# q and k read once in natural order, scores on four 64x64 tiles of TensorE, pooled scores on row tiles

## The chip, the cores and the metric

The kernel is one program on one core of a Trainium2 chip. A core has five engines that run lists of their own and meet through semaphores: TensorE (PE in the rows, with its weight loads as PEld), VectorE (DVE), ScalarE (ACT), GpSimd (POOL) and SyncE (SP), which issues every DMA here, one queue in order. Matmuls write PSUM, of which the kernel uses eight banks of 128 partitions by 512 fp32 columns. The metric is device time of one execution in microseconds, the median of several runs; lower is better.

## The reference

Attention of 8 batches, 8 heads, 576 positions, 64 dims, in two branches whose sum goes through a gated network. One branch averages q, k and v over groups of four positions and attends fully (144 x 144 scores); the other looks at a band of 7 keys around each query.

```python
q_d = q.reshape(B, H, Sd, 4, D).mean(axis=3)      # k_d, v_d alike; Sd = 144
out_up = np.repeat(sm_attn(q_d, k_d, v_d), 4, axis=2)
mask = np.abs(pos[:, None] - pos[None, :]) < 4
scores = np.where(mask, scale * np.matmul(q, k.transpose(0, 1, 3, 2)), -1e9)
out_local = np.matmul(softmax(scores), v)
x = (out_up + out_local) as (B * S, H * D)         # 4608 x 512
return (sigmoid(x @ w_gate) * (x @ w_val)) @ w_out # 512 -> 1536 -> 512
```

## The kernel before

A **unit** is one batch and two heads (32 units, four to a batch, numbered u = 0 to 31). A unit's attention is a chain of steps, each a small function in `unit_steps`:

- `prep2`: GpSimd sums groups of four columns of q and k (pooled q and k; k goes into a block tile `kdblk`, one half of partitions to a head, the rest zero).
- `s0`, `s1`: band scores. The 576 positions are cut into 10 blocks of 58 queries, each with 64 keys around it, and each block of each head is one 64x64x64 product in fp32, 20 to a unit, into two PSUM banks (tiles `s`). The host has laid q and k out twice: `qk`, in which the two partition halves hold even and odd blocks, cut and padded (a product of the lower half stands on rows and columns 0 to 63 of the array, one of the upper half on 64 to 127), and `qkd`, plain, with the two heads in the two partition halves, for pooling.
- `sm`, `a0`, `a1`, `v`, `x`: softmax, transposes and the product with v (tiles `x`). For the first six units (fp32, `plain`) v is copied by ScalarE into a block tile with zeros, and one 128x128x58 product serves a block of both heads. Later units use fp16 pairs and three passes.
- `d0`, `d1`, `dn`, `at`, `vd`, `od`: the pooled branch. `d0` and `d1` are one product each of pooled q (72 columns of it as weights, all 128 partitions) with `kdblk` (288 columns: both heads beside each other), tiles `sd`; after each, DVE takes row maxima and ScalarE two exponentials.

From a unit's output comes x. Batches 0 and 1 multiply it with w_gate and w_val as they are (`pg`, `pv`), while the weights are still being read, joined and split into fp16 pairs (`wload`, `wjoin`, `wsplit`); from batch 2 on seven products in place of eight are made from sums of weights (`pair`). `po` is the output product. All large products are fp16 in three passes of 288 columns.

**The order.** Every step has a place on one line, a number in the table `T` (`p0s0`, `m3d1` and so on); the steps are recorded in the order of their numbers, and a scheduler that knows the tiles then sets each engine's list. PSUM is two pools: five banks `mm` (products of the network, and everything of units 0 to 3) and three banks `att` (scores, pooled scores and transposes of later units). In units from 8 on the 20 band products are kept together; earlier they stand in groups of 12 and 8. While nothing else is to be done early, `awake` fills PE with idle products. Loads go through `load`, which keeps them in order on SP: for the first four units `qk`, mask, `qkd`, `vd` (pooled v), all four v, and so on by unit; `qk` has two buffers, `qkd` one (units 0 to 3 borrow room elsewhere).

Of the kernel before, what the change touches and what calls it, by code (L numbers as in the profile page):

```python
# [9 lines left out]
F16 = mybir.dt.float16  # L10
# [9 lines left out]
P = 128  # L20
# [5 lines left out]
R = 58  # L26
# [5 lines left out]
QR = 80  # L32
# [15 lines left out]
NSWAP = 8  # L48
NKD = 2
# [17 lines left out]
def attention_moe(ctx, tc, qk, qkd, v, vd, wg, wv, wo, mask, out):  # L67
# [53 lines left out]
    assert NRING * NBLOCK * KB + 4 * HN <= (NPC + 1) * WPC and 2 * XQ + 8 * HN <= (NPC + 1) * WPC and 3 * S + 8 * HN <= NST * 2 * WPC  # L121
# [18 lines left out]
    def borrowed(eng, i, n):  # L140
        t = borrow(i, n * P)
        eng.memset(t, 0.0)
        return t.rearrange("p (a b) -> p a b", a=n)

    vplain = [borrowed(nc.vector, 1, NBLK), borrowed(nc.gpsimd, 1, NBLK)]
    vdblk = [zeroed(nc.gpsimd, [P, NKC, P], F32, f"vdblk{i}") for i in range(2)]
    kdblk = [zeroed(nc.vector, [P, 2, SD], F32, f"kdblk{i}") for i in range(NKD)]
    adw = zeroed(nc.gpsimd, [QR, 2 * NKC * 2 * WIN], F32, "ad")
    ad = adw[:QM].rearrange("p (q c h k) -> p q c h k", q=2, c=NKC, h=2)
    ad16 = adw.bitcast(F16).rearrange("p (e q c h k) -> p e q c h k", e=2, q=2, c=NKC, h=2)  # L150
    vblk = cp.tile([P, 2, NBLK, P], F16, tag="vblk", name="vblk")
    vd16 = [t.rearrange("p c d -> p (c d)").bitcast(F16).rearrange("p (e c d) -> p e c d", e=2, c=NKC) for t in vdblk]
    flat = {id(vblk): vblk.rearrange("p t b c -> p (t b c)").bitcast(F32), id(adw): adw, **{id(t): t.rearrange("p c d -> p (c d)") for t in vdblk}}

    ones = cp.tile([P, 1], F32, tag="ones", name="ones")
    nc.vector.memset(ones, 1.0)
# [30 lines left out]
    def inv_scaled(dst, src, c):  # L187
        nc.vector.reciprocal(dst, src)
        nc.vector.tensor_scalar(out=dst, in0=dst, scalar1=c, scalar2=None, op0=ALU.mult)

    def absmax(dst, src):
        nc.vector.tensor_reduce(dst, src, axis=AX.X, op=ALU.max, apply_absolute_value=True)  # L192

    def split(hi, lo, src, sc):

        nc.scalar.activation(hi, src, AF.Copy, scale=sc)  # L196
        return nc.vector.scalar_tensor_tensor(out=lo, in0=src, scalar=sc, in1=hi, op0=ALU.mult, op1=ALU.subtract)  # L197


    mark = {}  # L200
# [157 lines left out]
    qkraw, qkdraw, vdraw = {}, {}, {}  # L358

    def load_qk(u):  # L360
        if 2 <= u < NPAIR:
            qkraw[u] = borrow(1, 2 * NJ * (R + WIN))
        else:
            qkraw[u] = raw.tile([P, 2 * NJ * (R + WIN)], F32, tag="qk", name=f"qk{u}", bufs=2)
        load(qkraw[u], qk[u])

    def load_qkd(u):
        if 1 <= u < NPAIR:
            qkdraw[u] = borrow(0, 2 * S)
# [15 lines left out]
    def first_loads():  # L385
        n = 0
        for u in range(NPAIR):
            load_qk(u)
            if u == 0:
                load(mk, mask)  # L390
# [773 lines left out]
```

## Time and profile before

| | us |
|---|---|
| median of 3 runs | 1016.58 (1010.73 to 1024.09) |
| profiled execution, its own time | 1018.99 |
| its span, first to last instruction | 1017.2 |
| first network product on PE | 63.4 |
| first product of batch 2's network | 340.5 |
| start of the last batch's network | 916.5 |

Before the first network product the attention of batch 0 and the first weights are prepared. From there to 150.4 us the network of batch 0 runs while the weights of the rest arrive; from 340.5 to 916.5 us five batches follow each other at about 115 us each; the last batch has no attention beside it.

### The profile page before, as it was taken

The page shows a single profiled execution, that of the slowest core. Times are in us where ns is not written, and L with a number is a line of the kernel's source. Part 1 is how long each engine was busy: PE and PEld are TensorE (multiplying, and loading weights), DVE is VectorE, ACT ScalarE, POOL GpSimd, SP SyncE. Part 2 cuts the span into 40 slices and gives each one's busy share as a digit, 9 for nine tenths or more (in the row PEclk, how much of TensorE's full clock was granted, in tenths as well). Part 3 has the DMA queues.
Part 4 walks back from the last instruction along what each step waited for, and adds up shares of the span by engine and source line. Part 5 has one row for each costly group of instructions (what it writes and reads, how often), then busy time and mean ns, then how long its engine had stood idle before and what let it go on. Part 6 is the DMA issues. An engine that isn't in the chain of part 4 may idle for free.

```text
span 1017.2 us, 23779 instructions
## 1 busy us (share of the span) xinstructions
PE 993.7 (98%) x9467; PEld 794.5 (78%) x9467; DVE 759.8 (75%) x1487; ACT 592.1 (58%) x1627; POOL 257.5 (25%) x309
## 2 busy tenths in 40 slices
PE   8999999999989999999999999999999999999998
PEld 6786677878778778878887777878778778887776
DVE  5968998576875899858895788857896588736850
ACT  5958778366763787535862676536863477322310
POOL 6400146523534322221402312221402311110000
PEclk9989999999999999999999999999999999999999
DMA  9548964333536557554855458555756455414501
GB/s 356 184 146 268 331 213 141 129 91 132 178 113 207 184 195 232 160 177 149 271 174 184 137 194 233 156 160 173 257 152 198 141 189 167 147 52 152 178 9 46
DMA packets 84735, 176.88 MB, mean 174 GB/s; under 512 B 44048, under 2 KB 50320, under 8 KB 84624
## 3 DMA queue, kind: packets, MB, share of 16 engines
q1 hardware_dynamic: 84624, 175.37, 52.7%
q8 instruction: 74, 1.21, 0.5%
q14 instruction: 37, 0.30, 0.1%
HBM read 147.03 MB, written 20.45 MB: 165 GB/s over the span
## 4 chain that ended last, share of the span: by engine, by line
PE 67%; DMA 12%; DVE 7%; ACT 5%; POOL 5%; issue 2%; SPq 1%; POOLq 0%; ACTq 0%; DVEq 0%
PE po L439 23%; PE pv L439 17%; PE pg L439 17%; DMA qkd<-in_qkd_dram 3%; PE s L502 3%; DMA v<-in_v_dram 2%; PE x L439 2%; PE sd L439 2%; POOL arena L840 2%; DMA wd<-arena 2%; PE od L439 1%; DMA arena<-in_wo_dram 1%; DMA at<-hl 1%; DMA arena<-in_wv_dram 1%; DVE arena L849 1%
## 5 line engine op out<-in xcount | busy, mean ns | idle before, releaser
L439 PEld LDWEIGHTS <-arena 128*128 128x128 f16 x4176 | 405.7, 98 | 118.2 <-ACT arena L196 4.4
L439 PE MATMUL po<-gq,wo 128*128 128x288 f16 x2304 | 290.5, 286 | 3.2 <-DVE gq L197 1.4
L439 PE MATMUL pg<-arena 128*128 128x288 f16 x2088 | 277.7, 288 | 5.9 <-ACT arena L196 3.5
L439 PE MATMUL pv<-arena 128*128 128x288 f16 x2088 | 274.3, 286 | 0.1
L439 PEld LDWEIGHTS <-wo 128*128 128x128 f16 x2304 | 223.8, 98 | 62.0 <-issue 3.0
L893 DVE TENSOR_TENSOR arena<-pv,arena 128x288 f32<-128x288 f32 x252 | 106.7, 451 | 27.0 <-PE pv L439 20.0
L537 ACT ACTIVATE t<-t,mx 128x64 f32<-128x64 f32 x300 | 75.4, 334 | 37.0 <-DVE mx L533 36.9
L419 POOL TENSOR_TENSOR qkd<-qkd 128x576 f32<-128x576 f32 x29 | 38.3, 1320 | 207.8 <-DMA qkd<-in_qkd_dram 207.8
L893 DVE TENSOR_TENSOR arena<-pg,arena 128x288 f32<-128x288 f32 x180 | 76.0, 449 | 10.7 <-PE pg L439 8.0
L196 ACT ACTIVATE vblk<-v,svb 64x640 f16<-64x640 f32 x52 | 42.9, 824 | 52.6 <-PE x L439 47.7
L554 ACT ACTIVATE t<-t,sm 128x64 f32<-128x64 f32 x250 | 62.3, 336 | 4.4 <-DVE sm L551 3.7
L813 ACT ACTIVATE arena<-po,osc 128x288 f32<-128x288 f32 x32 | 15.3, 496 | 71.7 <-PE po L439 71.7
L197 DVE SCALAR_TENSOR_TENSOR vblk<-v,svb,vblk 64x640 f16<-64x640 f32 x52 | 53.8, 1034 | 3.3 <-ACT vblk L196 2.2
L811 DVE TENSOR_SCALAR arena<-po,osc 128x288 f32<-128x288 f32 x32 | 16.3, 512 | 51.2 <-PE po L439 51.1
L714 POOL TENSOR_TENSOR arena<-arena 128x288 f32<-128x288 f32 x12 | 9.6, 796 | 171.3 <-DVE arena L689 171.3
L589 ACT ACTIVATE e<-sd,mxd 72x144 f32<-72x144 f32 x128 | 47.0, 370 | 6.1 <-POOL ad L614 5.0
L439 PE MATMUL sd<-kdblk,qks 128*72 128x288 f32 x128 | 42.7, 415 | 4.1 <-POOL kdblk L421 2.1
L502 PEld LDWEIGHTS s<-qk 64*64 64x64 f32 x1200 | 38.2, 135 | 8.2 <-issue 5.1
L502 PE MATMUL s<-qk 64*64 64x64 f32 x1200 | 43.4, 221 | 1.2 <-ACT e L589 0.9
L421 POOL TENSOR_TENSOR qks<-qkd 128x144 f32<-128x144 f32 x29 | 15.2, 525 | 113.3 <-PE sd L439 112.9
L521 DVE SCALAR_TENSOR_TENSOR t<-s,mk 128x256 f32<-128x256 f32 (+1 forms) x64 | 30.3, 484 | 14.9 <-PE s L502 14.8
L192 DVE TENSOR_REDUCE vm<-v 128x1 f32<-128x640 f32 x32 | 25.9, 812 | 19.7 <-DMA v<-in_v_dram 19.6
(147 smaller groups left out, 1400.5 us busy)
## 6 DMA issues: line engine op xcount, KB each, us to landing
arena<-wd SPq DMA_DIRECT2D x72, 896.0 KB, 4.6
qk<-in_qk_dram SPq DMA_DIRECT2D x30, 610.0 KB, 5.2
qkd<-in_qkd_dram SPq DMA_DIRECT2D x29, 576.0 KB, 5.5
vd<-in_vd_dram SPq DMA_DIRECT2D x29, 384.0 KB, 4.7
v<-in_v_dram SPq DMA_DIRECT2D x32, 320.0 KB, 4.9
arena<-in_wg_dram SPq DMA_DIRECT2D x12, 512.0 KB, 4.9
arena<-in_wv_dram SPq DMA_DIRECT2D x12, 512.0 KB, 4.6
arena<-in_wo_dram SPq DMA_DIRECT2D x12, 512.0 KB, 5.5
```

The lines of the kernel that those rows point to most:

```text
L192: nc.vector.tensor_reduce(dst, src, axis=AX.X, op=ALU.max, apply_absolute_value=True)
L196: nc.scalar.activation(hi, src, AF.Copy, scale=sc)
L197: return nc.vector.scalar_tensor_tensor(out=lo, in0=src, scalar=sc, in1=hi, op0=ALU.mult, op1=ALU.subtract)
L419: nc.gpsimd.tensor_tensor(out=x[:, :, 0:2], in0=x[:, :, 0:2], in1=x[:, :, 2:4], op=ALU.add)
L439: nc.tensor.matmul(o, w[a], x[c], start=first and i == 0, stop=last and i == len(pairs) - 1)
L502: return nc.tensor.matmul(o, qkraw[u][ps, g * R : g * R + WIN], kw[ps, g], start=True, stop=True)
L521: nc.vector.scalar_tensor_tensor(out=s["t"][:, j0:j1, :], in0=s["s", j0][:, : n * 2 * WIN].rearrange("p (a b) -> p a b", a=n), scalar=-QKS ...
L537: nc.scalar.activation(t[:, g], t[:, g], AF.Exp, bias=mx[:, g : g + 1], scale=-1.0, **(dict(accum_out=s["sm"][:, g : g + 1]) if fl("acs", ...
L554: nc.scalar.activation(t[:, g], t[:, g], AF.Copy, scale=sm[:, g : g + 1])
L589: nc.scalar.activation(s["e"][:, qb, h, :], pt[:QM, h * SD : (h + 1) * SD], AF.Exp, bias=mx[:, h : h + 1], scale=QKSCALE / 16, accum_out=s ...
L840: whole = nc.gpsimd.tensor_tensor(out=x.rearrange("p (f c) -> p f c", f=2), in0=home[k][:, 2 * p : 2 * p + 2, 0], in1=home[k][:, 2 * p : 2 ...
L893: eng.tensor_tensor(out=dst_, in0=x, in1=y, op=ALU.add)
```

## The change

**Loads.** `qk` is no longer read. `qkd` is loaded once a unit into a buffer with 13 columns of zero padding behind q and behind k, and serves pooling and band scores. Three such buffers go round. The order of the first loads is now a list of numbers in `T`: q of unit 0, mask, pooled v of unit 0, q of unit 1, two weights, and so on, with v last.

**Band scores.** Partition half is now the head, and the block's parity decides the output half, so the 20 products of a unit stand on all four 64x64 tiles of the array: rows by head, columns by parity. Each head has its own bank. They are kept together in all units.

**Pooled scores.** `kdblk` is gone. Pooled q and k stay side by side, and each head is a product of its own on 64 rows (72 columns of weights, 144 columns moving), two of each head, four to a unit, issued together in `d0` into two banks; the maxima and exponentials of head 0 are `d0`, those of head 1 `d1`.

**Pooling.** Two GpSimd instructions in place of four.

**Values.** In units 0 to 5 v is used as it is loaded: 20 products of 64x64 by 58 columns in place of 10 of 128x128, and no copies by ScalarE. The block tile for later units is zeroed once at the start instead of twice later.

**Places.** Most numbers of `T` differ. In the early units some work is on other engines: units 1 and 3 subtract their maxima on GpSimd and take one exponential (10 before), unit 0 does the reverse, and unit 0's division of the pooled branch goes from ScalarE to GpSimd.

```diff
     def load_qk(u):
-        if 2 <= u < NPAIR:
-            qkraw[u] = borrow(1, 2 * NJ * (R + WIN))
...
+        if NQK <= u < NPAIR:
+            qkraw[u] = padded(borrow(1, QKW))
         else:
-            qkdraw[u] = raw.tile([P, 2 * S], F32, tag="qkd", name=f"qkd{u}", bufs=1)
-        load(qkdraw[u], qkd[u])
+            qkraw[u] = qkbuf[u % NQK if u < NPAIR else (u - NPAIR) % NQK]
+        own(qkraw[u], u)
+        load(qkraw[u].rearrange("p (a c) -> p a c", a=2)[:, :, :S], qkd[u].rearrange("p (a c) -> p a c", a=2))
...
         def prep2():
-            sum4([(ALL, s["qd"], slice(0, SD))] + [(ps, s["kd"][ps, h], slice(SD, 2 * SD)) for h, ps in enumerate(HALVES)], x, fl("pr", u))
...
+            nc.gpsimd.tensor_tensor(out=y, in0=x[:, :, :, 0:2], in1=x[:, :, :, 2:4], op=ALU.add)
+            nc.gpsimd.tensor_tensor(out=s["qks"].rearrange("p (a g) -> p a g", a=2), in0=y[:, :, :, 0], in1=y[:, :, :, 1], op=ALU.add)
...
+        def s_four():
+            mine(qkraw[u], u)
+            for h in range(2):
+                s["s", h] = bank(f"s_{u}_{h}")
...
+            def one(h, hs, g, ps):
+                o = s["s", h][ps, g // 2 * WIN : (g // 2 + 1) * WIN]
+                a = g * R
+                return nc.tensor.matmul(o, qkraw[u][hs, a : a + WIN], qkraw[u][hs, QW + a : QW + a + WIN], start=True, stop=True).ins
...
+            run = [lambda x=(h, hs, 2 * j + par, ps): one(*x) for j in range(NJ) for h, hs in enumerate(HALVES) for par, ps in enumerate(HALVES)]
+            joined(run[2:] + run[:2])
...
+        def sd_products():
+            for h in range(2):
+                s["sd", h] = bank(f"sd_{u}_{h}")
+            return [lambda qb=qb, h=h, hs=hs: nc.tensor.matmul(
+                s["sd", h][:QM, qb * SD : (qb + 1) * SD], s["qks"][hs, qb * QM : (qb + 1) * QM], s["qks"][hs, SD:], start=True, stop=True).ins
+                for qb in range(2) for h, hs in ((1, HALVES[1]), (0, HALVES[0]))]
...
+            if plain:
+                for i0, i1 in CUT:
+                    o(i0, ALL)
+                joined([lambda i=i, ps=ps: nc.tensor.matmul(o(i, ps), vraw[u][ps, i], s["at"][0][ps, i, :R], start=True, stop=True).ins
+                        for i in [8, 9] + list(range(8)) for ps in HALVES])
```

PE, the band scores of unit 12 before (`po_1_2_0` is an output product of batch 1; a row with x8 is eight such products):

```order
L439 MATMUL po_1_2_0_4354<-gq_111,wo16_110 128x288
L439 MATMUL od_11_4323<-adt16_11_4320,vdblk1_121 128x144 x3
L502 MATMUL s_12_3_4330<-qk12_4150 64x64 x8
L502 MATMUL s_12_0_4329<-qk12_4150 64x64 x12
L439 LDWEIGHTS wo16_110
```

and the same place now:

```order
L424 MATMUL od_11_4326<-adt16_11_4324,vdblk1_119 128x144 x3
L460 MATMUL s_12_1_4333<-qk2_142 64x64 x2
L460 MATMUL s_12_0_4332<-qk2_142 64x64 x2
L460 MATMUL s_12_1_4333<-qk2_142 64x64 x2
L460 MATMUL s_12_0_4332<-qk2_142 64x64 x2
```

The number behind `s_12_` is now the head; head 1 and head 0 take turns, two products each (even and odd block). So it is in units 0, 4, 8 to 14, 16 to 18 and so on; in ten units (1, 2, 3, 5, 6, 7, 15, 19, 23, 27) ten products of head 1 stand ahead of ten of head 0.

PE, the pooled scores of units 14 and 15 now, with the band scores of unit 15 between them (before, `sd_14_0` and `sd_14_1` were one product each, 24 weight loads and products apart):

```order
L474 MATMUL sd_14_1_5194<-qks_14_5047 72x144
L474 MATMUL sd_14_0_5193<-qks_14_5047 72x144
L474 MATMUL sd_14_1_5194<-qks_14_5047 72x144
L474 MATMUL sd_14_0_5193<-qks_14_5047 72x144
...
L460 MATMUL s_15_1_5415<-qk2_142 64x64 x10
L460 MATMUL s_15_0_5414<-qk2_142 64x64 x10
...
L474 MATMUL sd_15_1_5516<-qks_15_5330 72x144 x2
...
L474 MATMUL sd_15_0_5515<-qks_15_5330 72x144 x2
```

In units 10, 15, 19, 23 and 27 the two heads' pooled products stand apart like those of unit 15, with three or six products of the network between them; in units 2, 3, 4 and 6 two of head 1 stand directly ahead of two of head 0; in the others they alternate.

## Rows read from the trace of the kernel before

**Rows 1.** Windows: stretch, its length, busy us by engine, clock, DMA share, GB/s.

```profile
0.00:63.40 63.40, 58.52 (x543) 48.00 (x544) 48.51 (x109) 45.90 (x138) 27.18 (x43) 0.92 0.64 238
63.40:150.40 87.00, 82.82 (x681) 62.37 (x680) 76.01 (x167) 66.87 (x160) 13.50 (x15) 0.96 0.77 263
150.40:340.50 190.10, 182.70 (x1807) 146.14 (x1806) 137.81 (x267) 117.37 (x338) 85.17 (x81) 1.00 0.43 138
340.50:916.50 576.00, 572.47 (x5650) 460.63 (x5649) 444.30 (x845) 341.12 (x964) 131.67 (x170) 1.00 0.56 179
916.50:1017.20 100.70, 97.16 (x794) 77.38 (x791) 53.17 (x101) 20.83 (x28) 0.00 (x0) 1.00 0.28 97
```

**Rows 2.** Waits of PE: us in total, times, longest.

```profile
PE sd L439 <- POOL kdblk L421: 2.1, 1, 2.1
PE sd L439 <- POOL qks L421: 1.3, 2, 0.7
```

**Rows 3.** Timeline of PE in batch 3: start, busy us, group.

```profile
480.65 0.65 PE L439 MATMUL sd<-kdblk,qks 128*72 128x288 f32 x2
481.13 0.90 PE L439 MATMUL pv<-arena 128*128 128x288 f16 x6
...
491.39 1.38 PE L502 MATMUL s<-qk 64*64 64x64 f32 x40
492.71 2.38 PE L439 MATMUL pv<-arena 128*128 128x288 f16 x18
...
496.39 0.90 PE L439 MATMUL od<-adt,vdblk 128*128 128x144 f32 x6
497.13 0.65 PE L439 MATMUL sd<-kdblk,qks 128*72 128x288 f32 x2
```

**Rows 4.** Timeline of PE, the first 12 band products of unit 0.

```profile
6.32 0.91 PE L502 MATMUL s<-qk 64*64 64x64 f32 x24
7.17 0.39 PE L88 MATMUL awake<-idle 128*128 128x256 bf16 x2
```

**Rows 5.** Windows of L502 alone: stretch, length, PE, PEld; (x) counts those in flight.

```profile
491.39:491.41 0.02, 0.01 (x2) 0.02 (x2) 1.00 0.85 358
...
491.49:491.51 0.02, 0.02 (x4) 0.02 (x5) 1.00 3.40 1434
491.51:491.55 0.04, 0.04 (x4) 0.04 (x6) 1.00 1.27 538
491.55:491.57 0.02, 0.02 (x6) 0.02 (x6) 1.00 1.70 717
491.57:491.61 0.04, 0.04 (x6) 0.04 (x6) 1.00 0.85 358
```

**Rows 6.** Timeline of PE, the value products of unit 4.

```profile
150.54 1.45 PE L439 MATMUL x<-at,vblk 128*128 128x58 f32 x12
151.82 0.27 PE L167 MATMUL mxt<-ident,m1o 128*1 128x128 f32 x1
...
152.31 1.04 PE L439 MATMUL x<-at,vblk 128*128 128x58 f32 x8
153.29 0.38 PE L172 MATMUL mxt<-mxg,ones 1*128 1x1 f32 x2
```

**Rows 7.** Timeline of the front: the first units' pooled chain.

```profile
7.90 1.15 POOL L419 TENSOR_TENSOR qkd<-qkd 128x576 f32<-128x576 f32 x1 [3.03 <-DMA qkd<-in_qkd_dram]
...
22.70 2.11 POOL L419 TENSOR_TENSOR gq<-gq 128x576 f32<-128x576 f32 x2 [3.17 <-DMA gq<-in_qkd_dram]
```

**Rows 8.** Windows of the front, columns as in rows 1.

```profile
10.00:20.00 10.00, 8.50 (x80) 6.01 (x81) 7.83 (x19) 8.47 (x23) 7.61 (x13) 0.83 1.03 415
20.00:30.00 10.00, 10.00 (x122) 8.62 (x122) 8.92 (x20) 9.25 (x38) 7.04 (x9) 1.00 1.01 404
```

**Rows 9.** ScalarE's groups from 0 to 63.4 us: busy, mean ns.

```profile
L481 ACT COPY wo<-v 64x640 f32<-64x640 f32 x8 | 5.8, 721 | 0.1
```

**Rows 10.** The page's DMA issues: count, KB each, us to landing.

```profile
qk<-in_qk_dram SPq DMA_DIRECT2D x30, 610.0 KB, 5.2
```

**Rows 11.** What touches the tiles `sd`: count, duration ns min/median/max.

```profile
L589 ACT ACTIVATE e<-sd,mxd x128: 355/370/387, 14.3 to 855.4; 72x144 f32<-72x144 f32 x128
L589 ACT ACTIVATION_READ_ACCUMULATOR e<-sd,mxd x128: 185/192/207, 14.6 to 855.7; 72x1 f32 x128
L586 DVE TENSOR_REDUCE mxd<-sd x64: 422/444/454, 13.6 to 851.4; 72x2 f32<-72x288 f32 x64
```

More of the change, by code (lines that the diff above doesn't have):

```diff
@@ L31 @@
 QM = SD // 2
-QR = 80
 KC = 48
@@ L47 @@
 NPLAIN = 6
-NSWAP = 8
-NKD = 2
+QW = NBLK * R + 6
+QKW = 2 * (QW + 3)
+NQK = 3
 QKSCALE = 1.0 / 8
@@ L469, in unit_steps @@
         VDB = vdblk[u % 2]
-        VB, VT = vblk, vplain[u % 2] if u < NPAIR else vblk
-        VBp = [VT] if u < NPAIR else in_parts(vblk, NBLK)
-        def take(t):
-            if t is vblk and u in (NPAIR, NPLAIN):
-                assert owner[id(t)] == "zero", (u, owner[id(t)])
-            own(t, u)
-        def plain_v():
-            take(VT)
-            for ps in HALVES:
-                nc.scalar.copy(VBp[0][ps, :, ps], vraw[u][ps])
         def bank(name):
@@ L487, in prep2 @@
         def prep2():
-            x = qkdraw[u].rearrange("p (g f) -> p g f", f=4)
-            s["qd"] = wk.tile([P, SD], F32, tag="qks", name=f"qks_{u}", bufs=1)
-            s["kd"] = kdblk[u % len(kdblk)]
-            own(s["kd"], u)
-            sum4([(ALL, s["qd"], slice(0, SD))] + [(ps, s["kd"][ps, h], slice(SD, 2 * SD)) for h, ps in enumerate(HALVES)], x, fl("pr", u))
-        def s_products(groups):
-            kw = qkraw[u][:, NQ:].rearrange("p (a b) -> p a b", b=WIN)
-            some = []
-            for j0, j1 in groups:
-                pt = s["s", j0] = bank(f"s_{u}_{j0}")
-                some += [(pt[ps, (g - 2 * j0) * WIN : (g - 2 * j0 + 1) * WIN], g, ps) for g in range(2 * j0, 2 * j1) for ps in HALVES]
-            def one(o, g, ps):
-                return nc.tensor.matmul(o, qkraw[u][ps, g * R : g * R + WIN], kw[ps, g], start=True, stop=True)
-            if not srun:
-                for x in some:
-                    one(*x)
-            else:
-                some = some[12:] + some[:12]
-                with tc.issue_after(one(*some[0]).ins), tc.high_priority():
-                    for x in some[1:]:
-                        one(*x)
@@ new lines, in joined @@
+        def joined(run):
+            with tc.issue_after(run[0]()), tc.high_priority():
+                for f in run[1:]:
+                    f()
+        def sd_products():
[4 more added lines that the diff above has]
+                for qb in range(2) for h, hs in ((1, HALVES[1]), (0, HALVES[0]))]
@@ L559, in vsplit @@
         def vsplit():
-            take(VT)
-            for par in range(2):
-                ps = slice(par * 64, par * 64 + 64)
-                split(VB[ps, 0, :, ps], VB[ps, 1, :, ps], vraw[u][ps], svb[ps, b : b + 1])
+            own(vblk, u)
+            for ps in HALVES:
+                split(vblk[ps, 0, :, ps], vblk[ps, 1, :, ps], vraw[u][ps], svb[ps, b : b + 1])
         def vdsum():
-            if u in (T["da"], T["da"] + 1):
-                zero(VDB)
-            take(VDB)
+            own(VDB, u)
@@ L670, in av_down @@
[L670 to L689 removed]
+                product(pt[:, :SD], [VDB[:, c]], [s["adt"][:, c]], c == 0, c == NKC - 1)
@@ new lines, in av_down, with av_local, o @@
+            s["od"] = wk.tile([P, SD], F32, tag="od", name=f"od16_{u}")
+            nc.scalar.activation(s["od"], pt[:, :SD], AF.Copy, **({} if plain else dict(scale=sxb[:, b : b + 1])))
+        def av_local():
+            pts = s["x"] = {}
+            CUT = ((0, 8), (8, NBLK))
+            for i0, i1 in CUT:
+                for i in range(i0, i1):
+                    pts[i] = i0
+            def o(i, ps):
+                i0 = pts[i]
+                if (i0, "pt") not in s:
+                    s[i0, "pt"] = mm(f"x_{u}_{i0}")
+                return s[i0, "pt"][ps, (i - i0) * R : (i - i0 + 1) * R]
+            if plain:
+                for i0, i1 in CUT:
+                    o(i0, ALL)
+                joined([lambda i=i, ps=ps: nc.tensor.matmul(o(i, ps), vraw[u][ps, i], s["at"][0][ps, i, :R], start=True, stop=True).ins
+                        for i in [8, 9] + list(range(8)) for ps in HALVES])
+            s["xs"] = xs2 if b >= 2 and u % 2 else xs1
+            assert b < 2 or all(("a", k, i) in done for k in "gvo" for i in range(NPC))
+            own(s["xs"], u)
+            for i0, i1 in CUT:
+                if not plain:
+                    mine(vblk, u)
+                    for i in range(i0, i1):
+                        product(o(i, ALL), [vblk[:, e, i] for e in range(2)], [s["at"][e][:, i, :R] for e in range(2)])
+                t0, t1 = i0 * R, min(i1 * R, S)
+                g0, g1 = t0 // 4, t1 // 4
+                nc.vector.tensor_tensor(
+                    out=s["xs"][:, t0:t1].rearrange("p (g f) -> p g f", f=4), in0=s[i0, "pt"][:, : t1 - t0].rearrange("p (g f) -> p g f", f=4),
+                    in1=s["od"][:, g0:g1].unsqueeze(2).to_broadcast([P, g1 - g0, 4]), op=ALU.add)
@@ L976, in at @@
         p = placed(u, k)
-        return max(p, placed(u - 1, "x") + (0.05 if k == "a0" else 0.1)) if k in ("a0", "a1") and u >= T["dt"] else p
+        if k in ("a0", "a1") and u >= T["dt"]:
+            p = max(p, placed(u - 1, "x") + (0.05 if k == "a0" else 0.1))
+        return p
     def placed(u, k):
```

197 lines of the change are left out of this document (55 added, 142 removed).

## The prediction

> **What bounds the kernel now.** I read the windows first [rows 1]. From 340.5 to 916.5 us PE is busy for 572.5 of 576.0 us at the full granted clock (1.00, 2.4 GHz), and from 150.4 to 340.5 us for 182.7 of 190.1. DVE, the next, has 444.3 of 576.0, and the DMA engines are at 0.56. So behind 150 us the end moves by what PE's own list loses or gains, and by little else. Ahead of it no single engine is full: up to 63.4 us DVE has 48.5 and ScalarE 45.9, and from 63.4 to 150.4 PE has 82.8 of 87.0 at a clock of 0.96 (a part at 1.2 GHz), DVE 76.0, with the DMA engines at 0.77. There a shorter list of any one engine is worth less than its length. The waits of PE that end with a pooling instruction are small [rows 2]: 2.1 and 1.3 us. The timeline of PE then gives what each step of a unit costs it, from the start of the step to the start of the next [rows 3].
>
> **Band scores.** 40 rows, two passes of each of the 20 products, take 491.39 to 492.71, 1.32 us [rows 3]; 24 rows take 6.32 to 7.17, 0.85 us [rows 4]. The difference, 0.47 us for 16 rows, is 29.4 ns a row, and 0.145 us is left that does not depend on the count: the price of going over to small tiles and back. Then I looked at how the rows start [rows 5]: the count in flight goes up by two, at about 491.40, 491.50 and 491.56, and stands still between. Two passes start together every 58.8 ns, so the two tiles used now do work beside each other. If four do, 40 passes are ten rounds of 58.8 ns: 0.59 + 0.145 = 0.73 us, 0.59 less per unit. If only two can, nothing is gained. Where head 1's ten products stand ahead of head 0's, only the two tiles of one row half are at hand; there I take no gain, and the loss if those two cannot overlap is one more 1.17 us a unit. In the stretch where PE sets the time (units 6 to 31; the scores of 4 and 5 fall into batch 0's network), 19 units alternate and unit 31 half: 19.5 x 0.59 = **11.5 us** (bounds: -7.0, from six units at 1.17, and 11.5). I take the upper one, because the rows show passes of different tiles starting together, and nothing in them shows that two is a limit.
>
> **Pooled scores.** Now two products, 480.65 to 481.13 and 497.13 to 497.61 (the other starts of that batch alike): 0.48 us each, 0.97 a unit [rows 3]. No row has 64-row tiles with 144 columns moving; the nearest is `od`, 144 columns on the whole array, six passes in 0.74 us, 0.123 each [rows 3]. Four products are eight passes: with both heads beside each other 4 x 0.123 + 0.145 = 0.64, a gain of 0.33; one after the other 8 x 0.123 + 0.145 = 1.13, a loss of 0.16. Five units have network products between the heads and pay the change of tiles twice: 0.98 + 0.29, a loss of 0.30. With two row halves overlapping, as the band scores do: 21 x 0.33 - 5 x 0.30 = **5.4 us** (bounds: -4.9 and 5.4).
>
> **Values.** Unit 4's products take 1.28 + 0.98 = 2.26 us [rows 6], unit 5's look alike. As 40 passes of small tiles, on the two diagonal tiles that the band scores use now, they cost 40 x 0.0294 + 0.145 = 1.32: 2 x 0.94 = **1.9 us**. Units 0 to 3 gain the same in the front, where PE is not the end.
>
> **Pooling.** PE's 3.4 us of waits [rows 2] are for `kdblk`, which is gone, and for `qks`, which now stands two instructions behind its load and not four: **2 us** (0 to 3.4). What GpSimd itself saves is hidden; it is busy for 131.7 of 576 us [rows 1].
>
> **The front.** Between 10 and 30 us the DMA engines are full (1.03 and 1.01, at 415 and 404 GB/s) [rows 8]. Four units' `qk` at 610 KB [rows 10], 2.44 MB, would be 5.9 us of that. Unit 0's pooling waited until 7.90 for the second load, and the third and fourth units' until 22.70 [rows 7]; now each unit has one load for both uses, and it stands ahead of v. ScalarE loses eight copies, 5.8 us [rows 9], and, net, nine short exponentials (units 1 and 3 take one in place of ten, unit 0 ten in place of one). DVE, though, loses only two memsets there, and more weight joins now stand ahead of the first network product. So the gain is between nothing (DVE's list sets it) and 10 us (half of DVE's 14.9 idle us up to 63.4, and part of the 4.2 that PE idles behind it); neither bound is near, and I take **5 us** at 150 us.
>
> **What is late next.** A unit now asks for two `att` banks at once for its pooled scores, where it asked for one and then another, and holds the second until `d1`. With three banks the next scores stand behind that. The waits on banks before are too small to stand in the rows; I take **2 us** off (0 to 20, see the rivals). In SP's queue a load goes away for every unit and none is moved ahead of a weight that PE needs sooner; three buffers let it start earlier. I cost that at nothing: it is covered by network products as long as these stand between load and use.
>
> **The sum.** 11.5 + 5.4 + 1.9 + 2 + 5 - 2 = 23.8 us. Against the profiled execution (1018.99, 1.8 us of it outside the span) that is 995.2; this execution is 2.4 us above the median of the runs, so as a median **993 us**, 2.3% less. The runs shown lie within 1.3% of each other; two per cent is about what a measurement of this kernel can tell from no change.
>
> **The rivals.** (1) *Two passes at a time is the limit.* A product's second pass must wait for its first, as both use the same tile. If passes start in the order of the list, only a second pass and the next product's first can overlap, however many tiles there are. For it: the pace of 58.8 ns is just one pass of 64 columns at the pace of `od`'s (0.123 x 64 / 144 = 54 ns) and a little more, so no more than two were ever needed to explain it. Against it: the first two rows start together and the next two 0.1 us later [rows 5]; in strict order the first pass would start alone. Then the band scores gain nothing, and pooled scores take five steps of 0.123 + 0.145 = 0.76, a gain of 0.21: 21 x 0.21 - 1.5 = 2.9. The sum is 2.9 + 1.9 + 2 + 5 - 2 = 9.8, **1007 us**. The Trainium skill speaks for this one: "TensorE: Matmul & The Clock Gate", Part 3 (under what overlaps and what doesn't), says that matmuls start and end in the order of the program, and that weight loads overlap matmuls in flight only where the row group differs. The trace's first two starts do not agree with the first half of that, and four tiles with shared row groups were not run, so it gets a chance of its own and not the forecast.
>
> (2) *The front gives more.* If DVE's first 10 us fill up, because scores of units 1 to 3 come at 8 to 15 us rather than at 15 to 30, the front's bound of 10 us is reached and batch 0's network flows without its gaps: 7 us more, **986 us**, with the rest as forecast. Against it: DVE has 8.9 of 10 us between 20 and 30 already [rows 8].
>
> (3) *Slower: the second pooled bank.* A head's eviction is one maximum of 0.44 us, a scaling, and two exponentials with their sums, 2 x (0.37 + 0.19) [rows 11]: 1.7 us and more. Where the next scores come before `d1` has done it, PE stands still at the head of its list, with the network's products queued behind. If each of the 26 units pays one such eviction, that is 26 x 1.7 = 44 us against gains of 25.8: 18 us slower, **1035 us**. It decides from 1.0 us a unit. Against it: in the order, 24 to 36 network passes (3 to 4 us) stand between most pooled scores and the next scores, and DVE is idle for a quarter of the time [rows 1].
>
> **How the numbers follow.** Forecast 0.47 (985 to 1000), rival 1 0.27 (1000 to 1012), rival 2 0.17 (974 to 988), rival 3 0.09 (1010 to 1040). The range takes in the forecast, rival 1 with its bounds and most of rival 2: 974 to 1014, which leaves out the far half of rival 3 and a tail on the other side. Faster by over 2% means under 996.2: three quarters of the forecast and all of rival 2, about 0.50; slower by over 2%, above 1036.9, is a part of rival 3, 0.05; within 2% 0.45.
>
> **What would show it.** Right: the 40 rows of `s` in 0.7 to 0.8 us in alternating units, with four starting together; eight `sd` rows in about 0.65; batches at about 112 us in place of 115; the first network product near 60 us. Wrong: rows of `s` still in pairs 58 ns apart, or PE waiting for DVE or ScalarE ahead of `s` or `sd` by more than a microsecond a unit, or a front that ends where it did.

## The result, and the profile after

The changed kernel took 1006.25 us (median of 20 runs, 997.0 to 1011.44) and the kernel before 1016.6 (20 runs): ratio 0.9898, 95% interval 0.987 to 0.9925. That is 10.4 us faster, 1.0%, where 993 us and 2.3% were forecast. It lies inside the range (974 to 1014), next to the figure of rival 1 (1007); the rows below show that rival 1's mechanism is not what happened. The profiled execution took 1004.63 us with a span of 1002.9; it lies 14.4 us below the one shown of the kernel before (1018.99), 4 more than the medians.

Windows of the changed kernel, cut at the same events as [rows 1] (first network product of batch 0, end of its network, first product of batch 2's network, start of the last batch's network; columns as there):

```profile
0.00:56.00 56.00, 50.21 (x639) 40.02 (x640) 46.76 (x115) 38.88 (x121) 27.53 (x37) 0.97 0.72 252
56.00:140.30 84.30, 78.51 (x692) 60.66 (x690) 75.15 (x168) 63.49 (x158) 18.81 (x16) 1.00 0.75 244
140.30:336.00 195.70, 182.79 (x1874) 144.40 (x1873) 139.85 (x270) 115.47 (x326) 70.97 (x64) 0.97 0.37 115
336.00:902.10 566.10, 563.39 (x5726) 452.00 (x5724) 433.30 (x844) 338.10 (x957) 114.26 (x128) 1.00 0.51 159
902.10:1002.90 100.80, 97.21 (x794) 77.41 (x792) 53.20 (x101) 20.85 (x28) 0.00 (x0) 1.00 0.29 97
```

Against [rows 1] the front ends 7.4 us earlier and batch 0's network 10.1. Then the third stretch, where PE had set the pace, gets 5.6 us longer (195.7 for 190.1) although its products got shorter; its clock is 0.97 in place of 1.00. Batch 2 starts only 4.5 us earlier. The five batches behind it take 566.1 us for 576.0, 9.9 less.

Timeline of PE in batch 3 of the changed kernel (start, busy us, group), the counterpart of [rows 3]:

```profile
454.57 0.81 PE L460 MATMUL s<-qk 64*64 64x64 f32 x40
455.31 2.38 PE L424 MATMUL pg<-arena 128*128 128x288 f16 x18
...
461.68 0.71 PE L474 MATMUL sd<-qks 64*72 64x144 f32 x8
462.33 1.64 PE L424 MATMUL pv<-arena 128*128 128x288 f16 x12
...
480.94 1.63 PE L460 MATMUL s<-qk 64*64 64x64 f32 x40
482.50 0.91 PE L424 MATMUL pg<-arena 128*128 128x288 f16 x6
```

From start to next start the alternating band scores cost 0.74 us, the pooled scores 0.65, and a unit with ten and ten 1.56. Windows over the band scores of 454.57 alone (stretch, length, PE, PEld, clock, DMA; (x) counts those in flight), the counterpart of [rows 5]:

```profile
454.56:454.60 0.04, 0.03 (x4) 0.03 (x4) 1.00 0.00 0
454.60:454.66 0.06, 0.06 (x4) 0.06 (x8) 1.00 0.00 0
454.66:454.70 0.04, 0.04 (x8) 0.04 (x12) 1.00 0.00 0
454.70:454.73 0.03, 0.03 (x8) 0.03 (x11) 1.00 0.00 0
454.73:454.76 0.03, 0.03 (x12) 0.03 (x12) 1.00 0.00 0
```

The count now goes up by four at a time, where it went up by two: four tiles run beside each other.

Where the third stretch lost its time, the waits of PE from 190 to 340 us show (us in total, times, longest), against [rows 2]:

```profile
PE po L424 <- ACT gq L186: 4.6, 1, 4.6
PE mxt L162 <- DVE mxg L161: 2.9, 1, 2.9
PE od L424 <- ACT adt L559: 2.0, 1, 2.0
PE sd L474 <- DVE t L482: 1.2, 1, 1.2
```

And around these waits, windows (columns as in rows 1):

```profile
280.00:290.00 10.00, 5.46 (x45) 4.37 (x44) 9.72 (x13) 4.47 (x7) 2.80 (x4) 0.96 0.29 104
290.00:300.00 10.00, 9.91 (x81) 6.98 (x81) 5.27 (x10) 2.80 (x5) 2.12 (x1) 0.70 0.47 166
...
310.00:320.00 10.00, 8.00 (x99) 6.33 (x97) 4.89 (x8) 4.84 (x14) 4.29 (x6) 1.00 0.65 222
...
330.00:340.00 10.00, 10.00 (x103) 7.33 (x102) 9.66 (x18) 7.20 (x22) 4.80 (x3) 0.83 0.18 33
```

Behind the waits of 4.6 us (to 290.1) and 2.9 us (to 329.2) part of the next 10 us ran at the lower level, 1.2 GHz; behind the wait of 2.0 us (to 313.25) the clock stayed at 1.00. By these rows the clock cost some 5.1 us more, an estimate: 10 us times what is missing to 1.00, that is 0.4, 3.0 and 1.7 us in the windows from 280, 290 and 330.

What PE waited for is seen in the timeline of the other engines (time in brackets: idle before, and who ended it). L779, L788, L791 and L792 are the four engine steps of `sums`, which makes batch 2's weight sums in one buffer: an add on GpSimd, four adds on DVE, a cast on ScalarE, a subtraction on DVE, then a write; twelve times.

```profile
278.06 2.12 POOL L779 TENSOR_TENSOR arena<-arena 128x1024 f32<-128x1024 f16 x1 [7.68 <-DMA wd<-arena]
280.22 1.93 DVE L788 TENSOR_TENSOR arena<-arena 128x256 f32<-128x256 f32 x2 [4.28 <-POOL arena L779]
288.88 0.44 DVE L723 SCALAR_TENSOR_TENSOR tanh<-tanh,pv 128x288 f32<-128x288 f32 x1
289.35 0.68 ACT L186 ACTIVATE gq<-tanh 128x576 f16<-128x576 f32 x1 [2.07 <-DVE tanh L723]
290.09 2.32 PE L424 MATMUL po<-gq,wo 128*128 128x288 f16 x9 [4.62 <-ACT gq L186]
...
311.64 1.04 ACT L791 CAST arena<-arena 128x1024 f16<-128x1024 f32 x1 [7.95 <-DVE arena L788]
312.60 0.51 ACT L559 COPY adt<-adt 128x432 f32<-128x432 f32 x1
...
322.48 2.06 DVE L788 TENSOR_TENSOR arena<-arena 128x256 f32<-128x256 f32 x4 [5.74 <-POOL arena L779]
328.99 0.19 DVE L161 TENSOR_SCALAR mxg<-ident,mxr 1x1 f32<-1x1 f32 x1
```

Each of PE's three long waits stands behind one of these: DVE idles 4.28 us for GpSimd, which waited for the previous sum's write, and comes late with the `tanh` that `gq` needs; ScalarE idles 7.95 us ahead of `adt`; DVE idles 5.74 us ahead of `mxg`. The first sum starts at 189.9 us, the last at 332.1.

### The profile page after: what moved, and what is told of

Same layout as the page of the kernel before. It is cut to its first block, busy times and chain, and to the rows that moved or that the text cites. A ratio compares the mean times of both kernels' runs of the same rounds, so it can differ in the third digit from the quotient of the medians.

```text
span 1002.9 us, 24111 instructions
## 1 busy us (share of the span) xinstructions
PE 972.1 (97%) x9715; PEld 774.5 (77%) x9715; DVE 748.3 (75%) x1495; ACT 576.8 (58%) x1588; POOL 231.6 (23%) x244
## 4 chain that ended last, share of the span: by engine, by line
PE 67%; DVE 12%; DMA 8%; ACT 7%; issue 3%; POOL 2%; SPq 0%; ACTq 0%; DVEq 0%; POOLq 0%
PE po L424 23%; PE pv L424 18%; PE pg L424 18%; DMA v<-in_v_dram 2%; DMA arena<-in_wg_dram 2%; PE s L460 2%; PE x L424 2%; ACT t L496 1%; PE sd L474 1%; PE od L424 1%; DVE vblk L187 1%; DVE arena L788 1%; DVE arena L832 1%; DMA wd<-arena 1%; DMA arena<-in_wv_dram 1%
## 5 line engine op out<-in xcount | busy, mean ns | idle before, releaser
L424 PEld LDWEIGHTS <-arena 128*128 128x128 f16 x4176 | 401.8, 98 | 111.8 <-issue 10.3
L424 PE MATMUL po<-gq,wo 128*128 128x288 f16 x2304 | 294.5, 289 | 5.7 <-ACT gq L186 4.6
L424 PE MATMUL pg<-arena 128*128 128x288 f16 x2088 | 274.5, 286 | 3.8 <-ACT arena L186 1.6
L750 DVE TENSOR_SCALAR arena<-po,osc 128x288 f32<-128x288 f32 x32 | 16.5, 514 | 86.2 <-PE po L424 63.4
L449 POOL TENSOR_TENSOR qkh<-qk 128x576 f32<-128x576 f32 x31 | 40.5, 1306 | 93.0 <-DMA qk<-in_qkd_dram 92.1
L407 POOL TENSOR_TENSOR vdblk<-vd 64x192 f32<-64x192 f32 x58 | 35.8, 617 | 88.0 <-PE od L424 84.9
L450 POOL TENSOR_TENSOR qks<-qkh 128x288 f32<-128x288 f32 x32 | 26.9, 840 | 113.8 <-PE sd L474 113.4
L632 ACT CAST arena<-arena 128x576 f16<-128x576 f32 (+1 forms) x24 | 21.9, 911 | 54.1 <-DVE arena L626 27.6
L405 POOL TENSOR_TENSOR vd<-vd 128x384 f32<-128x384 f32 x29 | 26.1, 901 | 88.9 <-DMA vd<-in_vd_dram 88.9
L633 DVE TENSOR_TENSOR arena<-arena 128x576 f16<-128x576 f32 (+1 forms) x24 | 28.3, 1180 | 23.4 <-ACT arena L632 23.3
L779 POOL TENSOR_TENSOR arena<-arena 128x1024 f32<-128x1024 f16 x12 | 26.1, 2171 | 59.5 <-DMA wd<-arena 51.1
## 6 DMA issues: line engine op xcount, KB each, us to landing
qk<-in_qkd_dram SPq DMA_DIRECT2D x31, 576.0 KB, 6.2
```

Of the source, the lines that this page charges most:

```text
L405: nc.gpsimd.tensor_tensor(out=x[:, :, 0:2], in0=x[:, :, 0:2], in1=x[:, :, 2:4], op=ALU.add)
L407: nc.gpsimd.tensor_tensor(out=o, in0=x[ps, g, 0], in1=x[ps, g, 1], op=ALU.add)
L424: nc.tensor.matmul(o, w[a], x[c], start=first and i == 0, stop=last and i == len(pairs) - 1)
L449: nc.gpsimd.tensor_tensor(out=y, in0=x[:, :, :, 0:2], in1=x[:, :, :, 2:4], op=ALU.add)
L450: nc.gpsimd.tensor_tensor(out=s["qks"].rearrange("p (a g) -> p a g", a=2), in0=y[:, :, :, 0], in1=y[:, :, :, 1], op=ALU.add)
L633: eng.tensor_tensor(out=dst_[:, :, 1], in0=src, in1=dst_[:, :, 0], op=ALU.subtract)
```

## The experiments

**Theory 1**: steps of the sums, waiting at the head of the in-order lists of DVE, ScalarE and GpSimd, hold up PE's next inputs, and there the gain was lost. **Theory 2**: PE's own list sets the end there too, and the waits were chance. **Theory 3**: the numbers in `T` merely place steps badly. N is the stretch from the first network product of batch 1 to that of batch 2, with its granted clock. All experiments but before_again had 5 rounds beside the kernel before. Of tight only the times are used.

| run | median us | ratio to before, 95% | N us | clock |
|---|---|---|---|---|
| before (the trace shown) | 1016.6 | | 130.7 | 1.00 |
| after | 1006.25 | 0.9898 [0.987, 0.9925] | 138.2 | 0.96 |
| control | 1008.23 | 0.9929 [0.9901, 0.9958] | 133.9 | 0.96 |
| dose_early | 1013.91 | 0.9978 [0.9954, 1.0002] | 148.5 | 0.95 |
| dose_late | 1019.4 | 1.0031 [1.0005, 1.0058] | 139.3 | 0.96 |
| no_sums | 986.91 | 0.9721 [0.9686, 0.9757] | 121.2 | 1.00 |
| before_nosums | 1012.41 | 0.9976 [0.9953, 0.9999] | 125.5 | 1.00 |
| before_again | 1014.26 (1 run) | | 130.0 | 1.00 |
| early_sums | 1009.79 | 0.9932 [0.9902, 0.9962] | 139.2 | 0.96 |
| late_sums | 1005.86 | 0.9906 [0.987, 0.9943] | 141.8 | 0.95 |
| old_places | 1007.25 | 0.9921 [0.9894, 0.9948] | 140.5 | 0.95 |
| v_places | 1007.82 | 0.992 [0.9892, 0.9949] | 139.9 | 0.96 |
| sums_pool | 1019.55 | 1.004 [1.0017, 1.0062] | 132.3 | 0.97 |
| zfree | 999.3 | 0.9843 [0.9811, 0.9875] | 132.5 | 0.99 |
| before_z | 1024.44 | 1.0084 [1.0057, 1.0111] | 137.1 | 0.98 |
| zfree_spread | 998.75 | 0.9823 [0.9796, 0.985] | 131.2 | 0.99 |
| ten | 1006.99 | 0.9921 [0.9893, 0.995] | 136.7 | 0.98 |
| tight | 1016.68 | 1.0013 [0.9985, 1.0041] | | |
| tight_z | 1007.98 | 0.9927 [0.9899, 0.9956] | 131.7 | 0.97 |

**control, dose_early, dose_late: is PE's list the bound?** The two doses add, at numbers of the order inside batch 1's or batch 3's network,

```diff
+    for i in range(12):
+        add(200 + 6.0 * i, lambda: awake(8))     # dose_late: 444
```

control: 

> The changed kernel once more, unedited. Theory 1 (the chain of weight sums): the twelve sums of weights for batch 2 (GpSimd adds, DVE four adds, ScalarE casts, DVE subtracts, a DMA writes, one buffer for all) stand one behind the other from 190 to 342 us, and DVE and ScalarE wait in their lists for it, with PE's next inputs queued behind. Then PE waits in batch 1's output product in every execution, for 7 to 12 us in sum, and batch 2's network starts at 334 to 338 us although batch 1's network ends near 281. Theory 2 (PE's list alone): those waits were chance of one execution; batch 2 would start at 323 to 328 us, the time being near 995. Median by theory 1 1002 to 1010 us.

dose_early: 

> 96 idle products on PE, in 12 groups of 8, among batch 1's network products (about 200 to 280 us). A product is 256 columns at 0.107 us, so PE's list grows by 10.2 us there. Theory 1 (the chain of weight sums sets when batch 2 can start): PE's waits in batch 1's output product take the added time up, batch 2 starts at most 3 us later, and the end moves by 0 to 3 us. Theory 2 (PE's list sets the end there too): the end comes 9 to 11 us later.

dose_late: 

> The same 96 idle products, among batch 3's network products (about 450 to 525 us), where the rows show PE busy throughout. Both theories: the end comes 9 to 11 us later. If it does not, PE's list is not the bound there either, and the terms of the sum for the later units were paid by something else.

The loss is no chance, though its size varies: N was 133.9 in control and 139.3 in dose_late, whose edit lies behind it. In control PE did not wait for `gq`, and its waits in batch 1's output product were 5.5 us, fewer than the 7 to 12 expected. dose_late cost 11.2 us against control, about what both theories said. dose_early cost 5.7, between the theories. In its trace N grew to 148.5, by 9 to 15 us, and PE still waited 10.3 us in it (11.4 in the changed kernel): there the added time was not taken up by the waits; the stretch behind N was some 3 us shorter (664.0 us for 666.9). So the sums are no fixed wall that PE runs into; the waits come wherever PE is. That form of theory 1 falls.

**no_sums, before_nosums, before_again: what do the sums cost each kernel?**

```diff
-        whole = nc.gpsimd.tensor_tensor(
...
-        with tc.issue_after(whole):
...
+        nc.sync.dma_start(wd[r][:, 12 * P :], home[k][:, 2 * p : 2 * p + 2].rearrange("p f e c -> p (f e c)"))
+        wready.add(r)
+        return
```

GpSimd's add and what stands behind this `return` (the four adds, the cast, the subtraction, the write of the result) are left out; the weights themselves are written in place of the sums.

no_sums: 

> The sums of weights are left out (what GpSimd, DVE and ScalarE compute for them; their bytes are still written, from the weights themselves, so the seven products of batches 2 to 7 are taken with wrong weights in four of them). Theory 1: no chain, PE does not wait in batch 1's output product, batch 2 starts at 322 to 328 us in place of 336, and the end comes 8 to 14 us sooner. Theory 2: the end moves by less than 3 us.

before_nosums: 

> The kernel before without what GpSimd, DVE and ScalarE compute for the sums of weights (bytes are still written; four of seven products have wrong weights). In the changed kernel leaving them out took 21 us off the end. Theory 1, if the sums cost the kernel before as much: 15 to 22 us sooner than the kernel before. Theory 1 in the form that a shorter list of PE pays more for them, and theory 3: 5 to 11 us sooner, since the stretch of batch 1's network (130.7 us) has only 7 us in it beyond PE's own products.

before_again: 

> The kernel before, unedited, for a second trace. The stretch from the first network product of batch 1 to that of batch 2 is 129 to 133 us, as in the first (130.7), if that is a property of the kernel; 134 to 139 us if the first trace was a lucky one, in which case the change lost nothing there.

Windows of N in the changed kernel and in no_sums, then in before_nosums (columns as in rows 1):

```profile
197.80:336.00 138.20, 126.74 (x1229) 99.30 (x1228) 96.23 (x168) 79.86 (x224) 51.18 (x41) 0.96 0.40 121
197.70:318.90 121.20, 121.20 (x1229) 97.20 (x1228) 64.52 (x120) 71.62 (x217) 27.18 (x30) 1.00 0.33 91
```

```profile
207.60:333.10 125.50, 124.44 (x1214) 99.71 (x1213) 64.89 (x122) 75.77 (x233) 25.72 (x33) 1.00 0.35 109
```

Without sums PE of the changed kernel has no gap in N: 121.2 us is its bare list. With them, the profiled execution has 11.4 us of waits and some 5.1 of lower clock more, which makes 137.7 of its 138.2. The kernel before paid for the same sums 130.0 to 130.7 less 125.5, some 5 us. At the end the sums cost the changed kernel 19 to 21 us (8 to 14 were expected) and the kernel before 2.6 to 4.2 (5 to 11 by the lower of its expectations). Between the two kernels without sums lie 1012.41 - 986.91 = 25.5 us: the forecast sum was 23.8. It does not come out term by term, though. Of the 27.8 us between the two spans 9.9 lie ahead of N, where 5 were forecast, 4.3 in N, and 13.6 in the five batches, which in before_nosums took longer than with the sums (578.8 us; 576.0 and 573.7 in the two traces of the kernel before). Theory 2 falls. What these two runs leave out is more than waiting: DVE also has 32 us less to do in N (64.5 for 96.2), and the writes in SP's queue no longer wait.

**early_sums, late_sums, old_places, v_places: bad places?**

```diff
-S0=2.49
+S0=-6.01      # early_sums;  late_sums: 7.26, as before
-vv=-8.33, vvs=2.29, vmm=1.85, vmms=1.91
+vv=-11.21, vvs=2.0, vmm=-4.48, vmms=2.56      # v_places
```

old_places has the numbers from batch 1's attention on as in the kernel before; the front and the joining of weights keep the changed kernel's.

early_sums: 

> One number of the order changed: all twelve sums stand 8.5 us earlier. Theory 1: the sums compete with batch 0's output product instead; batch 2's start moves by less than 4 us either way. Theory 3 (places): it moves by 5 us or more.

late_sums: 

> The same number as in the kernel before (7.26 in place of 2.49 behind the start of batch 1): the sums stand 4.8 us later. Theory 3 (the sums were placed badly by the change): the stretch from the start of batch 1's network to batch 2's goes back to the 131 us of before, the end comes 5 to 8 us sooner. Theory 1: no gain; 0 to 6 us later, since the last sums come later still.

old_places: 

> The changed kernel with the places (the numbers of the order) that the kernel before had for everything from batch 1's attention on; the front keeps its new places, and loads, products and pooling are the changed kernel's. Theory 3 (places: the new numbers put steps of batch 2's preparation where PE waits for them): the stretch from the first network product of batch 1 to that of batch 2, 134 to 139 us in the unedited changed kernel, falls to 125 to 130 us, and the end comes 5 to 10 us sooner. Theory 1 (the twelve sums hold up the lists, whatever the places): 134 us or more, the end within 3 us.

v_places: 

> Only the places of the loads of v and of the maxima over v (from batch 2 on) go back to the numbers of the kernel before, some 3 and 6 us earlier. If the wait of PE for the maximum over batch 2's v (3 us in each of three traces) comes from these places: that wait goes, with the stretch of lower clock behind it, and the end comes 3 to 5 us sooner. If it comes from DVE standing behind a step of the sums (theory 1): the wait stays above 1.5 us and the end moves by less than 2 us.

None of the four brought N below 139 us or the end out of the intervals of the unedited kernel. Theory 3, as a matter of these numbers, falls; the front's numbers were not tried. PE's wait for `mxg`, the maximum over v, stayed at 3.1 us in v_places with the maximum placed 6 us earlier: DVE came late to it all the same.

**sums_pool, zfree, before_z, zfree_spread: a shorter chain.** sums_pool turns `nc.vector` into `nc.gpsimd` in the four adds. zfree gives the result room of its own, so that the next sum need not wait for the write:

```diff
-        z = x.bitcast(F16).rearrange("p (s e c) -> p s e c", s=4, e=2)
...
+        zf = home["o"][:, 6::7].rearrange("p f e c -> p f (e c)")
+        z = zf.rearrange("p f (s e c) -> p f s e c", s=2, e=2)
...
```

sums_pool: 

> The four adds of each weight sum are on GpSimd in place of DVE (48 instructions); nothing is left out. Theory 1 (the lists of DVE and ScalarE are held up by steps of the sums, with PE's inputs queued behind): DVE no longer waits for GpSimd's first add and loses 48 x 0.42 = 20 us of its own work between 190 and 342 us, so the stretch from the start of batch 1's network to that of batch 2's, 134 to 139 us in three executions of the changed kernel, 121 without sums, falls to 122 to 130, and the end comes 4 to 14 us sooner. Theory 3 (the sums only stand in bad places of the order, and which engine adds is of no matter): within 3 us. Against both: GpSimd, which pools q, k and v as well, becomes the late one and the end comes up to 6 us later.

zfree: 

> Nothing is left out. The result of each weight sum gets room of its own (two unused slots of the third weight), so that GpSimd's add of the next sum need not wait until the result is written to memory, only until DVE's four adds have read. Theory 1, as the traces now put it: the chain of twelve sums (142 to 153 us, some 12.5 each, of which 6.2 is work on engines and 3 the write) ends 5 to 6 us behind the start of batch 2's network in five traces of the changed kernel and of the kernel before, and holds that start back. Then the chain gets shorter by up to 12 x 3 us, the waits of PE in batch 1's output product fall from 9 to below 4 us, batch 2's network starts at 322 to 331 us in place of 336 to 342, and the end comes 5 to 14 us sooner. Rival (the chain follows PE and is not waited for as a chain; what costs is DVE's and ScalarE's time for it): within 3 us.

before_z: 

> The kernel before with the same room for the results of the weight sums. Leaving its sums out altogether took 2.6 us off it, and its stretch from batch 1's network to batch 2's has 7 us beyond PE's own products, 2 without sums. So the shorter chain can give it 0 to 3 us. Then the change itself is worth about 13 us between two kernels whose chain is short, in place of 8 to 10 between the two as they were. If the chain theory is wrong and the room helps both kernels alike (writes, DVE), it becomes 6 to 10 us faster.

zfree_spread: 

> The changed kernel with the room for the sums' results, and the sums spread over the whole stretch (10.5 in place of 9.17 between them in the order). With the room alone the chain ended at 285 us, 45 us before batch 2 needed it, and PE waited for DVE among batch 1's network products (2.9, 1.8 and 1.5 us) while the sums were dense. If that density is what is left of the cost: the stretch of 132.5 us falls to 126 to 130 and the end comes 2 to 6 us sooner than with the room alone (993 to 997 us). If not: within 2 us of it.

Timeline of GpSimd in zfree, the second and the last sum:

```profile
203.75 2.13 POOL L779 TENSOR_TENSOR arena<-arena 128x1024 f32<-128x1024 f16 x1 [3.60 <-DVE sme L418]
...
276.08 2.13 POOL L779 TENSOR_TENSOR arena<-arena 128x1024 f32<-128x1024 f16 x1 [5.88 <-DVE arena L788]
```

The last sum starts at 276.1 in place of 332.1, no wait of PE in N is longer than 1.8 us, the clock there is 0.99, and the end comes 7 to 9 us sooner than in the changed kernel: with nothing left out, theory 1 in its form of held-up lists stands for this part of the 19 to 21 us. N stays 11 us above the bare list, and no run tells how much of that is waiting and how much the time of the steps themselves; spreading the sums did not change it (998.75 us). (The 2.9 us that the expectation of zfree_spread names is the sum of three waits, the longest 1.0.) zfree and zfree_spread beat both kernels, zfree_spread with an interval clear of that of the changed kernel.

The other two show how little such an edit carries over. In sums_pool N fell too, to 132.3, but the last sum started at 338.3 us in place of 332.1 and the price turned up in batch 2's network, so that the end came 11 to 13 us later, more than any expectation allowed (waits of PE from 330.5 to 425 us):

```profile
PE s L460 <- ACT e L535: 5.2, 1, 5.2
PE pv L424 <- DVE tanh L832: 2.2, 2, 1.5
PE s L460 <- ACT od L596: 2.1, 1, 2.1
```

The first is the wait of rival 3: scores held up until the exponentials of a pooled bank are done. In before_z the room made the kernel 8 us slower: N 137.1, with the longest wait of PE behind GpSimd's pooling, which stands behind a sum in its list (waits of PE in N, then GpSimd's timeline):

```profile
PE sd L439 <- POOL qks L421: 3.9, 1, 3.9
```

```profile
257.13 2.12 POOL L840 TENSOR_TENSOR arena<-arena 128x1024 f32<-128x1024 f16 x1 [4.37 <-DVE arena L849]
259.22 1.42 POOL L421 TENSOR_TENSOR qks<-qkd 128x144 f32<-128x144 f32 x1
```

The expectation of 0 to 3 us gained was wrong: between kernels with a short chain lie 25.1 us, not 13, because one of them suffers from it.

**ten, tight, tight_z: the order of the products.** ten issues all of head 1's band products ahead of head 0's; tight alternates both kinds of score strictly in every unit (each product issued behind the one ahead); tight_z is tight with zfree's room.

```diff
-            joined(run[2:] + run[:2])
+            strictly(run[2:] + run[:2])      # tight; ten: by head, then by block
-                joined(sd_products())
+                strictly(sd_products())      # tight alone
```

ten: 

> In every unit the ten band products of head 1 stand ahead of the ten of head 0, so that at any time only the two tiles of one row half are at hand. If four tiles work beside each other, as the rows of the changed kernel show (40 passes in 0.74 us alternating, 1.14 in the units that stood ten by ten with no wait between), each of 14.5 units behind 336 us pays 0.40 more, 5.8 us, and four units ahead of it 1.6 that may be waited away: 5 to 8 us later at the end. If two passes at a time were the limit (rival 1 of the prediction): no change.

tight: 

> Band products alternate strictly between the heads in every unit, and the four pooled products too. From the rows: 5 units with pooled products apart pay 1.28 in place of 0.65 (3.2 us), four units with ten and ten pay 1.14 to 2.17 in place of 0.75 (3.4 us). If these are all real savings of PE's list: batches 2 to 6 take 560 us in place of 566, 4 to 6 us sooner at the end. If the wait for a second bank is only moved (rival): within 2 us.

tight_z: 

> Both edits. By theory 1 and the rows of the band and pooled products they act in different stages and add: 9 to 18 us sooner than the changed kernel, 990 to 998 us. If either falls, the other alone is left.

PE in ten (timeline, then windows over the same band scores alone, as above):

```profile
455.73 1.21 PE L460 MATMUL s<-qk 64*64 64x64 f32 x40
456.87 0.30 PE L424 MATMUL pg<-arena 128*128 128x288 f16 x1
```

```profile
455.72:455.76 0.04, 0.03 (x2) 0.03 (x2) 1.00 0.00 0
455.76:455.83 0.07, 0.07 (x2) 0.07 (x4) 1.00 0.00 0
455.83:455.86 0.03, 0.03 (x4) 0.03 (x6) 1.00 0.00 0
...
455.89:455.92 0.03, 0.03 (x6) 0.03 (x6) 1.00 0.00 0
```

A unit costs 1.14 us, in pairs again, and yet the end did not move (1006.99 us against 1006.25 and 1008.23; the five batches took 568.3 us for 566.1 and 567.0). Of the 5.8 us expected, 1.3 to 2.2 came. In ten the pooled products of units 15, 19, 23 and 27 stand together (0.65 where they cost 1.28, some 2.5 us in all), and the units which in the changed kernel stood ten by ten and waited for a second bank (1.48, 1.56 and 2.17) do not wait, 1.8 us: together they give back most of the loss. Why the scheduler's lists fall out so is not shown. tight did not get both: the median rose by 8 us against control. In the trace of tight_z the front takes longer:

```profile
61.67 2.37 PE L424 MATMUL pg<-arena 128*128 128x288 f16 x18
```

That is 5.7 us later than in the changed kernel. Its five batches take 562.8 us, and zfree's, without the strict order, 563.9: of the 4 to 6 us expected there 1 came, and the front took more. tight's expectation was wrong, and with it tight_z's sum; what holds the front back under the strict order was not taken apart.

## Why the prediction was wrong, point by point

- **Band scores**: right. 0.74 us for an alternating unit, where 0.73 was worked out; four passes start together, ten times in (0.74 - 0.145) us, every 59 ns. Rival 1 (two at a time) is refuted by the counterpart of [rows 5], though its time was the nearest: 1007 came of another loss. Its page of the Trainium skill, "TensorE: Matmul & The Clock Gate", Part 3, in its list of what overlaps, lets weight loads overlap matmuls in flight only where the row group differs; in ten, with two tiles of one row half, the loads of the next two passes stand beside two matmuls in flight (0.07 us with two matmuls and four loads), so the trace does not bear that limit out (the ends of matmuls are modelled in it). Another page of the Trainium skill, "TensorEngine Tiling (Array Packing)", Tiling Modes, says that tiles load and multiply independently; with that the trace agrees (counts of 4, 8 and 12 in [rows 5]'s counterpart). Ten and ten, taken as 1.32 us, cost 1.14 where nothing was waited for, and 1.48 to 2.17 in those three of the four such units of the five batches in which the second head waited for a bank until ScalarE's exponentials were done.
- **Pooled scores**: right, 0.65 for 0.64; apart, twice 0.64, for 1.27.
- **Values**: right. The 40 passes of small tiles of unit 4 take 1.30 us, for 1.32.
- **Pooling and the second bank**: PE no longer waits for pooling in N. PE's waits ahead of `s` for the exponentials of a pooled bank are 1.2 us in all, and the four units of ten and ten cost 1.8 more than 1.14 each by such waits (0.6 of it among the 1.2), close to the 2 forecast; rival 3 did not come, though sums_pool shows it can. From 336 us on the terms give 9.1 (15.5 units at 0.59) + 4.1 (16 at 0.33 less 4 at 0.30) - 2 = 11.2 us; 9.9 were measured, and 6.7 between the second traces of the two kernels (573.7 in before_again, 567.0 in control).
- **The front**: 10.1 us at the end of batch 0's network in the traces shown, the upper bound and rival 2's condition, where 5 were forecast. Between the second traces it is 3.7 (148.5 us in before_again, 144.8 in control), so the size is not settled by them. Of the 10.1 us 4.5 were left at the start of batch 2.
- **The step that failed** is in the first paragraph: "behind 150 us the end moves by what PE's own list loses or gains, and by little else". It rests on a busy share of 182.7 of 190.1 us [rows 1], which tells how full PE was and not how late its feeders were. For the changed kernel it does not hold from 198 to 336 us: the sums of weights, which the change does not touch and the prediction does not mention, cost 13 to 18 us there (N of 133.9 to 139.3 us less 121.2) where they had cost 5. Without sums in either kernel the total comes out as forecast (25.5 us for 23.8), in part by luck: the front gave about 5 us more than its term, and PE's shorter list behind it about 1 less, counting as gain some waits that before_nosums has in the five batches. The list of what is late next looked at banks and loads, and not at the other work in the lists of DVE and ScalarE.
- **Open**: why the same sums hold up the changed kernel's lists more. Not the numbers in `T` from batch 1's attention on (four runs), and not that PE comes earlier (dose_early). The waits of the sums' steps show where the kernels differ, in the changed kernel (from 200 to 340 us), then in the kernel before (from 205):

```profile
POOL arena L779 <- DMA wd<-arena: 51.1, 9, 10.5
ACT arena L791 <- DVE arena L788: 18.4, 6, 8.0
DVE arena L788 <- POOL arena L779: 17.5, 7, 5.7
```

```profile
POOL arena L840 <- DMA wd<-arena: 36.8, 8, 10.2
DVE arena L849 <- POOL arena L840: 18.7, 8, 4.2
ACT arena L852 <- DVE arena L849: 4.4, 1, 4.4
```

DVE waits for GpSimd's adds about as long in both, but ScalarE's casts wait 18.4 us for DVE's adds where they waited 4.4; over all twelve sums it is 20 to 24 us in eight traces of the changed kernel (after, control, the two doses, early_sums, late_sums, v_places, ten), and 4.4 in before_again. It is not the whole price: in old_places the casts wait 11.4 us, and N is as long (140.5). Why DVE's adds come late to ScalarE, and what SP's queue adds, in which the writes of the sums stand for DVE ahead of later loads (67 us in the changed kernel, 62 before), no run here takes apart.

## What to carry to other kernels

A busy share near one says that an engine has little idle time, not that its feeders have slack: before counting a gain on it, look in the lists of the feeding engines for steps that wait for something slow, a write to memory above all, with its inputs queued behind. To find such a price, leave the suspected work out of both kernels; the difference between the two runs without it is what the change is worth by itself, and it too has to be looked at stage by stage. And when a measured time falls on a rival's number, look for its mechanism in the rows before believing it.

## What the runs showed of the hardware

Four 64x64 tiles of TensorE run fp32 passes of 64 columns beside each other: in the changed kernel four start every 59 ns. Two tiles that share a row half run beside each other too: in ten the count in flight goes up by two, 60 ns apart (455.83 and 455.89).

Waits of PE of up to 1.4 us left the granted clock of N at 1.00 in the kernel before, and a wait of 2.0 us was followed by 1.00 in the changed kernel; behind waits of 4.6 and 2.9 us it fell to 1.2 GHz for part of the next 10 us (0.70 and 0.83 on average). By these rows a wait of 4.6 us cost about 8, an estimate (4.6 + 0.4 + 3.0).
